# Making the negated DFT tables on GpSimd from the finished tables, behind the loads of batch 0

## The chip, the cores and the metric

The kernel runs on one core of a Trainium2 chip. Times are device microseconds of one execution of the whole program, as median of several executions. Before the change it was 611.16 us (610.72 to 611.26, 3 runs). Engines: PE is TensorE, PEld its weight loads, DVE is VectorE, ACT is ScalarE, POOL is GpSimd, SP issues DMAs.

## The reference

```python
# q, k, v: 8 batches, 12 heads, 448 positions, 64 per head
scores = scale * np.matmul(q, k.transpose(0, 1, 3, 2))
attn   = np.matmul(np.maximum(scores, 0.0) ** 2 / S, v)      # relu squared, no softmax
x      = attn.transpose(0, 2, 1, 3).reshape(B, 448, 768)
X      = np.fft.fft(np.fft.fft(x, axis=1), axis=2)
u      = x + np.real(X)
un     = (u - mean) / np.sqrt(var + 1e-06)                   # over the 768 channels
out    = u + np.maximum(un @ w_ch1, 0.0) @ w_ch2             # w_ch1: 768 x 3072
```

## The kernel before

Both Fourier transforms are matmuls with tables of cosines and sines, which the kernel makes itself in its first 30 us: a sequence table `seq` (128 x 2 x 2 x 240), its negated sine `nseq`, three channel tables `chan[m]` (128 x 2 x 386) and their negated sine halves `chan_neg`. DVE reduces the angles, ACT takes the sines. I call "stage 0" the stretch in which this goes on beside the attention of batch 0 and its first transform.

The kernel is not written in the order in which it runs. Each piece is a generator that asks for time on an engine, `need(engine, duration, dependencies, buffers)`. A scheduler on the host with a model of the durations lets them go in the order of their modelled starts, and that order is what is emitted for every engine. A change of one `need` can therefore reorder all engines.

```python
def build_dft():
    ...
    def turns(f, g, cols, rows, n, i):                 # the "reductions", on DVE
        r = work.tile([128, 2 * KH], mybir.dt.int32, name="dftr", ...)
        nc.vector.tensor_scalar(r[:, :n], cols, rows, None, op0=ALU.mult)
        nc.vector.scalar_tensor_tensor(f, cols, rows, r[:, :n], op0=ALU.mult, op1=ALU.subtract)
        nc.vector.scalar_tensor_tensor(g, f, -1.0, f, op0=ALU.mult, op1=ALU.max)
    def sine(dst, y, n, e, sign=1, bias=zero_t):
        e = yield need("ACT", act(n), [e + LATENCY["DVE"]])
        nc.scalar.activation(dst, y, AF.Sin, bias=bias, scale=sign * 2.0 * math.pi)
        dft_ready.t = e + LATENCY["ACT"]
    ...
    yield from sine(seq[:, 1, :, :]..., f[:, :2 * SX], 2 * SX, e)
    yield from sine(nseq...,            f[:, :2 * SX], 2 * SX, e, -1)      # negated: a third sine
    for m in range(3):
        e = yield need("DVE", 1.5, [indices_ready])
        y = work.tile([128, 4 * KH], FP32, name="dfty", ...)
        turns(...)
        yield from sine(chan[m][:, 0, :], y[:, 0:2 * KH], 2 * KH, e, -1, halfpi)
        yield from sine(chan[m][:, 1, :], y[:, 2 * KH:], 2 * KH, e)
        e = yield need("DVE", 0.3, [dft_ready])                           # negated: on DVE
        nc.vector.tensor_scalar(chan_neg[:, m], chan[m][:, :, KH:], -1.0, None, op0=ALU.mult)
        dft_ready.t = e + LATENCY["DVE"]
```

DVE's other work in stage 0 is the attention itself: it copies transposed q and k out of PSUM (`qkT`), squares ACT's relu of the scores in place, and makes two "folds" of every block of the result. The last two kinds read two operands from SBUF (a square reads its operand twice); the two `scalar_tensor_tensor` of the reductions above do so as well. Squares and folds are:

```python
nc.vector.tensor_tensor(r, r, r, op=ALU.mult)                                    # square
nc.vector.tensor_tensor(f[:, 0, :], x[:, 0:NS], x[:, XH:XH + NS], op=ALU.add)    # folds
nc.vector.tensor_tensor(f[:, 1, :], x[:, 0:NS], x[:, XH:XH + NS], op=ALU.subtract)
```

TensorE gets filler matmuls with zeros (tile `warm`) where the model thinks that it would idle. In `first_channels` the folds are multiplied with the channel tables.

Of the kernel before, what the change touches and what calls it, by code (L numbers as in the profile page):

```python
# [12 lines left out]
ALU = mybir.AluOpType  # L13
# [46 lines left out]
LATENCY = {"PE": 0.28, "ACT": 0.18, "DVE": 0.16, "POOL": 0.2, "SP": 0.1}  # L60
# [53 lines left out]
def need(eng, dur, deps=(), bufs=(), ok=None):  # L114
    return eng, dur, list(deps), list(bufs), ok


def mm(n):
    return n / 2400 + 0.006


def act(n):
    return n / 1200 + 0.2
# [14 lines left out]
def kernel(  # L138
# [9 lines left out]
    nc = tc.nc  # L148
# [8 lines left out]
    KH = D // 4 + 1  # L157
# [5 lines left out]
    SX = 240  # L163
# [19 lines left out]
    sch = Streams()  # L183
# [51 lines left out]
    seq = const.tile([128, 2, 2, SX], BF16, name="seqm")  # L235
    nseq = work.tile([128, 2, SX], BF16, name="nseq", tag="qs", bufs=1)
    chan = [const.tile([128, 2, 2 * KH], BF16, name=f"chan{m}") for m in range(3)]

    chan_neg = work.tile([128, 3, 2, KH], BF16, name="channeg", tag="xn", bufs=1)
    dft_ready, indices_ready = Cell(), Cell()  # L240

    def build_dft():
        row, col, col2 = drow, dcol, dcol2

        def turns(f, g, cols, rows, n, i):

            r = work.tile([128, 2 * KH], mybir.dt.int32, name="dftr", tag=f"pc{TC[i][0]}", bufs=1)
# [9 lines that stand above are left out]
        e = yield need("DVE", 0.3, [indices_ready])  # L257
        nc.vector.tensor_scalar(row[:, 0:2], row[:, 0:2], 1.0 / S, None, op0=ALU.mult)
        nc.vector.tensor_scalar(row[:, 4:7], row[:, 4:7], 1.0 / D, None, op0=ALU.mult)

        e = yield need("DVE", 2.1, [indices_ready])
        f = work.tile([128, 4 * KH], FP32, name="dfty", tag="u", bufs=2)
        g = work.tile([128, 4 * KH], FP32, name="dfty", tag="u", bufs=2)
        for i in range(2):
            turns(f[:, i * SX:(i + 1) * SX], g[:, i * SX:(i + 1) * SX], col[:, 0:SX], row[:, i:i + 1], SX, i)
        yield from sine(seq[:, 0, :, :].rearrange("p a s -> p (a s)"), g[:, :2 * SX], 2 * SX, e, -1, halfpi)
        yield from sine(seq[:, 1, :, :].rearrange("p a s -> p (a s)"), f[:, :2 * SX], 2 * SX, e)
        yield from sine(nseq.rearrange("p a s -> p (a s)"), f[:, :2 * SX], 2 * SX, e, -1)

        for m in range(3):  # L270
            e = yield need("DVE", 1.5, [indices_ready])
            y = work.tile([128, 4 * KH], FP32, name="dfty", tag="u1" if m < 2 else "o", bufs=2)
            turns(y[:, 2 * KH:], y[:, 0:2 * KH], col2, row[:, 4 + m:5 + m], 2 * KH, m % 2)
            yield from sine(chan[m][:, 0, :], y[:, 0:2 * KH], 2 * KH, e, -1, halfpi)
            yield from sine(chan[m][:, 1, :], y[:, 2 * KH:], 2 * KH, e)
            e = yield need("DVE", 0.3, [dft_ready])
            nc.vector.tensor_scalar(chan_neg[:, m], chan[m][:, :, KH:], -1.0, None, op0=ALU.mult)
            dft_ready.t = e + LATENCY["DVE"]


    GRP = 4 * R * HG * Dh * 4
# [155 lines left out]
    first_folds, f_ready, first_scores, first_mixed = [], [Cell() for _ in range(MC)], Cell(), Cell()  # L437
# [507 lines left out]
    def first_channels(i, ms):  # L945

        n0, n1 = TC[i]
        for m in ms:
            e = yield need("PE", 4 * mm(KH), [f_ready[m], dft_ready] + ([first_scores] if i else []),
                           [BS] if i and m == 0 else [])  # L950
            if i and m == 0:
                first_pps[i] = BS.take()
            for t in range(2):
                parts = [(0, 2 * KH, chan[m][:, t, :])] if m < 3 else \
                    [(0, KH, chan[m - 3][:, t, 0:KH]), (KH, 2 * KH, chan_neg[:, m - 3, t, :])]
                for c0, c1, tab in parts:
                    nc.tensor.matmul(first_pps[i][:n1 - n0, t, c0:c1], lhsT=first_folds[m][:, t, n0:n1], rhs=tab,  # L957
                                     start=(i == 1 and m == 0), stop=(m == MC - 1 and c1 == 2 * KH))
        if m < MC - 1:
            sch.add(first_channels(i, [MC - 1]), (0, 0))  # L960
        else:
            first_chan[i].t = e
            if all(c.t for c in first_chan):
                BXN.free.append(e)
# [170 lines left out]
    with tc.manual_schedule():  # L1135
        small_constants()
        sch.engine.update(POOL=0.5, DVE=0.8)

        sch.add(loading(), (0, 4))
        sch.add(build_dft(), (0, 0.5))  # L1140
        sch.add(turning(), (2, 2))
        sch.add(ffns(), (4, 0))
        sch.add(mixes(), (1, 1))
        sch.add(attention(0), (0, 0))
        for i in range(2):
            sch.add(first_channels(i, range(MC - 1)), (5, 5))
        sch.add(attentions(), (3, 3))
        sch.add(warming(), (9, 9))
        sch.run()
# [30 lines left out]
```

## Time and profile before

| | before |
|---|---|
| median of 3 runs | 611.16 us |
| span of the profiled run | 610.0 us |
| TensorE busy | 98% |
| DVE busy between 16 and 32 us | 15.45 of 16 us |
| first square on ACT starts (used below as the start of stage 0) | 9.68 us |
| first transform is copied out (tile `pc`, used as its end) | 41.05 us |

The prediction shows and reads the lines of this profile. In a timeline line the columns are start, time in us, engine, source line, operation, tiles, shapes, count and, in brackets, the idle time before it and what ended it. Two marks from ACT's timeline matter later: the copy of the first transform, and the first relu of the feed-forward layer (`hT`).

```profile
41.05 1.02 ACT L994 CAST pc<-psS 128x772 bf16<-128x772 f32 x1 [1.00 <-PE psS L957]
...
57.73 0.49 ACT L1063 ACTIVATE hT<-psF 128x384 bf16<-128x384 f32 x1 [2.33 <-PE psF L1090]
```

### The profile page before, as it was taken

What the parts mean: (1) busy time and instruction counts of PE and PEld (TensorE: products, weight loads), DVE (VectorE), ACT (ScalarE), POOL (GpSimd) and SP (SyncE); (2) the same over time, 40 slices, a digit from 0 to 9 for tenths busy, and PEclk for the clock granted to TensorE, in tenths of its full rate; (3) what the DMA queues carried; (4) which work ended last, traced back from release to release, by engine and by line L of the source; (5) the groups of instructions that cost most, each with busy time, mean ns of one, the idle gap of its engine ahead of it and who ended that gap; (6) DMA issues with size and microseconds to landing.
All of it is one profiled execution on the core that took longest, in us unless ns stands there. A gap on an engine that the chain in (4) does not pass through costs nothing.

```text
span 610.0 us, 10248 instructions
## 1 busy us (share of the span) xinstructions
PE 597.8 (98%) x4044; PEld 330.6 (54%) x4063; DVE 331.7 (54%) x767; ACT 315.6 (52%) x470; POOL 126.8 (21%) x175
## 2 busy tenths in 40 slices
PE   8998999999999999999999999999999999999997
PEld 6566556544455565555445565555445565554464
DVE  5966776965576768555744368545742447110011
ACT  5965772488555668536763167635782247114300
POOL 8432031411142124211420115210410004000000
PEclk9998999999999999999999999999999999999999
DMA  9999998965938995976496775985461225320022
GB/s 125 207 209 228 207 179 126 203 118 101 148 120 166 197 166 168 172 137 120 158 140 115 134 126 173 167 156 96 146 134 61 86 51 177 102 94 23 0 78 78
DMA packets 125216, 82.22 MB, mean 135 GB/s; under 512 B 76272, under 2 KB 113168, under 8 KB 125168
## 3 DMA queue, kind: packets, MB, share of 16 engines
q0 software_dynamic: 40320, 34.07, 35.3%
q1 hardware_dynamic: 84848, 47.50, 32.1%
q8 instruction: 32, 0.52, 0.3%
q14 instruction: 16, 0.13, 0.1%
HBM read 62.91 MB, written 26.69 MB: 147 GB/s over the span
## 4 chain that ended last, share of the span: by engine, by line
PE 84%; DVE 6%; ACT 5%; SPq 2%; issue 1%; DMA 1%; DVEq 0%; ACTq 0%
PE psF L1108 32%; PE psF L1090 31%; PE psF L524 7%; PE psS L538 6%; PE psS L982 2%; PE psS L1130 2%; ACT sq L558 2%; DVE stats L864 1%; PE psS L832 1%; ACT un L878 1%; SPq L923 1%; DMA o<-ubot 1%; PE psS L957 1%; PE psF L421 1%; ACT hT L1063 1%
## 5 line engine op out<-in xcount | busy, mean ns | idle before, releaser
L1090 PE MATMUL psF<-unT,w 128*128 128x384 bf16 (+1 forms) x1134 | 228.4, 353 | 2.2 <-ACT hT L1063 1.1
L558 ACT ACTIVATE sq<-psS 112x896 bf16<-112x896 f32 x192 | 165.3, 915 | 116.2 <-PE psS L538 116.2
L1108 PE MATMUL psF<-w,hT 128*128 128x384 bf16 (+2 forms) x1343 | 224.8, 326 | 0.1
L1108 PEld LDWEIGHTS <-hT 128*128 128x128 bf16 x1344 | 129.3, 98 | 92.4 <-issue 8.8
L1090 PEld LDWEIGHTS <-w 128*128 128x128 bf16 x1152 | 109.5, 98 | 111.6 <-issue 15.4
L1063 ACT ACTIVATE hT<-psF 128x512 bf16<-128x512 f32 (+1 forms) x180 | 98.2, 547 | 98.8 <-PE psF L1090 97.7
L564 DVE TENSOR_TENSOR sq<-sq 112x896 bf16<-112x896 bf16 x192 | 115.4, 619 | 48.5 <-ACT sq L558 46.9
L1071 DVE TENSOR_TENSOR o<-psF,o 128x384 f32<-128x384 f32 (+2 forms) x56 | 31.0, 554 | 109.8 <-PE psF L1108 108.5
L445 DVE TENSOR_SCALAR xT<-psF 128x224 bf16<-128x224 f32 x48 | 18.7, 390 | 74.7 <-PE psF L524 74.7
L538 PE MATMUL psS<-qkT 64*112 64x448 bf16 x384 | 52.6, 367 | 0.6 <-ACT qkT L426 0.4
L300 POOL DMA_DIRECT2D vn<-in_v_dram x24 | 17.3, 720 | 172.7 <-PE psF L524 154.1
L524 PE MATMUL psF<-sq,vn 112*64 112x448 bf16 x384 | 45.5, 358 | 1.4 <-DVE o L1071 0.5
L852 POOL TENSOR_TENSOR u<-tp,xn 128x385 f32<-128x385 f32 (+1 forms) x14 | 17.3, 1236 | 105.1 <-DVE tp L843 91.6
L538 PEld LDWEIGHTS <-qkT 64*112 64x112 bf16 x384 | 20.4, 125 | 27.9 <-issue 22.7
L878 ACT ACTIVATE un<-u,nmr,rstd 128x768 bf16<-128x768 f32 (+1 forms) x28 | 28.2, 1021 | 6.7 <-DVE nmr L873 6.7
L524 PEld LDWEIGHTS <-vn 112*64 112x64 bf16 x384 | 18.3, 109 | 23.1 <-issue 14.5
L864 DVE BATCH_NORM_STATS2 stats<-u 128x6 f32<-128x384 f32 (+1 forms) x56 | 28.1, 540 | 0.0
L900 POOL DMA_INDIRECT ubot<-u,back x16 | 16.8, 1048 | 43.3 <-DVE sq L564 27.5
L1130 PE MATMUL psS<-warm 128*128 128x126 bf16 (+1 forms) x210 | 18.9, 242 | 1.3 <-DVE warm L215 1.3
L300 POOL DMA_DIRECT2D qn<-in_q_dram x21 | 15.3, 728 | 23.1 <-DVE sq L564 9.2
L900 POOL DMA_INDIRECT nbot<-un,back x12 | 11.7, 972 | 35.6 <-ACT un L878 31.9
L452 DVE TENSOR_SCALAR xT<-psF 128x224 bf16<-128x224 f32 x47 | 18.0, 384 | 0.0
(119 smaller groups left out, 363.5 us busy)
## 6 DMA issues: line engine op xcount, KB each, us to landing
out_dram<-o SPq DMA_DIRECT2D x27, 384.0 KB, 2.6
vn<-in_v_dram POOLq DMA_DIRECT2D x24, 224.0 KB, 4.5
qn<-in_q_dram POOLq DMA_DIRECT2D x21, 224.0 KB, 6.3
kn<-in_k_dram POOLq DMA_DIRECT2D x21, 224.0 KB, 6.9
w<-in_moe_w_ch_dram POOLq DMA_DIRECT2D x12, 384.0 KB, 13.5
w<-in_moe_w_ch_dram POOLq DMA_DIRECT2D x4, 1152.0 KB, 23.4
utop<-u SPq DMA_DIRECT2D x8, 384.0 KB, 2.6
o<-utop SPq DMA_DIRECT2D x8, 384.0 KB, 3.5
```

The lines of the kernel that those rows point to most:

```text
L300: nc.gpsimd.dma_start(out=t, in_=src[b, hs].rearrange("h (p j) d -> p h (j d)", j=4))
L524: nc.tensor.matmul(av[h * Dh:(h + 1) * Dh, 0:S], lhsT=vn[:, c, h0 + h, :], rhs=sq[:, h, :], start=(c == 0), stop=(c == 3))
L538: nc.tensor.matmul(sc[:R, h, 0:S].rearrange("k (c q) -> k c q", c=4), lhsT=kT[ps, m % 2, c, :], rhs=qT[ps, m % 2], start=True, stop=True)
L558: nc.scalar.activation(r, sc[:R, :, 0:S], AF.Relu)
L564: nc.vector.tensor_tensor(r, r, r, op=ALU.mult)
L864: nc.vector.bn_stats(stats[:n, hf, :], u[:n, hf * (D // 2):(hf + 1) * (D // 2)])
L878: nc.scalar.activation(un[:n], u[:n], AF.Identity, bias=nmr[:n, i:i + 1], scale=rstd[:n, i:i + 1])
L1063: nc.scalar.activation(h[:, 0:N], ph[:, 0:N], AF.Relu)
L1071: nc.vector.tensor_tensor(o[:, hs], pc[:, 0:w], o[:, hs], op=ALU.add)
L1090: nc.tensor.matmul(ph[:, 0:N], lhsT=w1_sb[m][hf][:, jj * 128:(jj + 1) * 128], rhs=unT[:, m, 0:N], start=(m == 0), stop=(m == MC - 1))
L1108: nc.tensor.matmul(pc[:, 0:w], lhsT=hT[j][:, c * 128:(c + 1) * 128], rhs=w2_sb[j // 6][:, j % 6, hs], start=(j == 0), stop=(j == JC - 1))
L1130: nc.tensor.matmul(first_pps[0][:, t, c0:512], lhsT=warm[:, 0:128], rhs=warm[:, c0:512], start=not begun, stop=False)
```

## The change

The intent is to take a sine from ACT and three negations from DVE, both close to full in stage 0, and give them to POOL. POOL makes all four negated tables from the finished ones, not earlier than 18 us of the model, when the loads of batch 0 have been issued. Four cells keep the matmuls with the channel tables from being planned before.

```diff
+    negs_ready = [Cell() for _ in range(4)]
+    def negate(dst, src, t):
+        e = yield need("POOL", 0.55, [t, 18.0])
+        nc.gpsimd.tensor_scalar(dst, src, -1.0, None, op0=ALU.mult)
+        [c for c in negs_ready if c.t is None][0].t = e + LATENCY["POOL"]
 ...
-        yield from sine(nseq.rearrange("p a s -> p (a s)"), f[:, :2 * SX], 2 * SX, e, -1)
+        sch.add(negate(nseq, seq[:, 1], dft_ready.t), (1, 1))
 ...
-            e = yield need("DVE", 0.3, [dft_ready])
-            nc.vector.tensor_scalar(chan_neg[:, m], chan[m][:, :, KH:], -1.0, None, op0=ALU.mult)
-            dft_ready.t = e + LATENCY["DVE"]
+            sch.add(negate(chan_neg[:, m], chan[m][:, :, KH:], dft_ready.t), (1, 1))
 ...   # in first_channels
-            e = yield need("PE", 4 * mm(KH), [f_ready[m], dft_ready] + ([first_scores] if i else []),
+            e = yield need("PE", 4 * mm(KH), [f_ready[m], dft_ready] + negs_ready + ([first_scores] if i else []),
```

## The prediction

> **What bounds the kernel now.** I read the page first, then the windows of its first hundred microseconds (the change touches only tables made there), then the chain of waits and the timelines of those microseconds.
>
> ```profile
> PE 597.8 (98%) x4044; PEld 330.6 (54%) x4063; DVE 331.7 (54%) x767; ACT 315.6 (52%) x470; POOL 126.8 (21%) x175
> ...
> L1130 PE MATMUL psS<-warm 128*128 128x126 bf16 (+1 forms) x210 | 18.9, 242 | 1.3 <-DVE warm L215 1.3
> ```
>
> TensorE is busy 98% of 610 us, so only what shortens TensorE's queue, or a wait in front of it, counts. But 210 of its matmuls multiply zeros: fillers (tile warm) that the kernel's own list scheduler puts where its model thinks TensorE would idle. In the first 41 us a busy TensorE is therefore no proof that it is the bound; nor, once emitted, are fillers free: they keep their place in the queue.
>
> The windows of stage 0 (attention of batch 0 and its first transform); columns are stretch, length, then busy us and count of PE, PEld, DVE, ACT, POOL, then clock, DMA share, GB/s:
>
> ```profile
> 8.00:16.00 8.00, 7.41 (x126) 5.39 (x120) 6.51 (x13) 7.31 (x11) 6.73 (x24) 1.00 1.30 163
> 16.00:24.00 8.00, 7.60 (x83) 4.34 (x82) 7.66 (x20) 7.23 (x11) 4.58 (x10) 1.00 1.31 204
> 24.00:32.00 8.00, 7.99 (x87) 4.43 (x85) 7.79 (x21) 7.13 (x10) 2.11 (x4) 1.00 1.09 213
> 32.00:41.00 9.00, 8.91 (x112) 6.00 (x111) 6.20 (x15) 5.20 (x7) 3.67 (x5) 1.00 1.08 211
> ```
>
> From 16 to 32 us DVE is busy 15.45 of 16 us, ACT 14.36, TensorE 15.59 with fillers: three engines nearly balanced, so taking work from one gives only what the next lets through. The chain of waits in time order shows where ACT and DVE carry the end:
>
> ```profile
> 9.68 3.34 ACT sq L558 x4
> 13.01 1.02 ACT chan L254 x2
> 14.03 0.02 issue
> 14.05 0.27 DVE channeg L277
> 14.32 0.41 DVE dftr L248
> ...
> 15.97 0.55 DVE qkT L426
> ```
>
> From 9.68 to 16.52 the chain runs over ACT, one negation on DVE (the very work that moves), the next table's reductions, and a copy. From 16.56 on it is TensorE almost without a break until 34.89, one ACT wait of 0.93 us, and TensorE again to 41.02.
>
> **What the Trainium skill says.** "SBUF — State Buffer", section "Who interferes with whom": DVE and GpSimd share a port pair as an exclusive lock; a DVE instruction with two SBUF inputs contends with a GpSimd instruction that reads SBUF, and the loser waits. The trace agrees:
>
> ```profile
> 14.75 0.62 DVE L249 SCALAR_TENSOR_TENSOR dfty<-dcol,drow,dftr 128x386 f32<-128x386 f32 x1
> 14.86 0.62 POOL L231 TENSOR_SCALAR backv<-backv 128x1 f32<-128x1 f32 x1
> 15.41 0.56 DVE L250 SCALAR_TENSOR_TENSOR dfty<-dfty 128x386 f32<-128x386 f32 x1
> 15.56 0.46 POOL L232 TENSOR_TENSOR backv<-backv 128x1 f32<-128x1 f32 x1
> 16.09 0.18 POOL L233 CAST back<-backv 128x1 int32<-128x1 f32 x1
> ```
>
> One column on POOL takes 0.62 us, ending at 15.48, just after the DVE instruction that ends at 15.37; the next takes 0.46, ending at 16.02 after DVE's 15.97; alone one takes 0.18. Here POOL lost; it can as well be DVE that loses.
> "GPSIMD Engine Reference", section 4.1, calls one-input elementwise work on GpSimd "roughly line-rate". The trace agrees: a 128x768 scale-and-shift there takes 0.98 us.
> "TensorE: Matmul & The Clock Gate", section "What's actually happening": the clock halves after an idle window of about 3.4 us, windows free-running. In windows of 3.413 us the trace has, right after a window with TensorE busy 1.68 of 3.41 us (51.09 to 54.50), exactly one at half clock:
>
> ```profile
> 54.50:57.91 3.41, 3.21 (x24) 0.50 1.24 206
> ```
>
> **The change part by part.**
> Removed from ACT: the third sine of the sequence tables, 0.68 us by its row, about 0.6 by the spacing of starts. It lay just before ACT's first squares, but those started at 9.68 when the scores ended at 9.65, so its end (9.48) held nothing up: 0 us there.
> Removed from DVE: three negations of 0.254 to 0.265 us, some 0.2 us each by spacing, 0.6 us in all, in the stretch where DVE is 97% busy. The first is on the chain (0.27 us), and so is its wait for ACT's chan sines.
> Added to POOL: four negations. From 0.98 us for 768 columns and 0.18 for one, about 1.04 ns a column: 0.68 us (480 columns) and three of 0.58 (386), 2.4 us. In the built kernel POOL's queue is: three w loads, two negations, three loads, one, three loads, one, the rest. Before, POOL idled ahead of those loads 0.51, 0.64, 0.64, 0.63, 1.31, 1.31, 1.38, 1.31 us, waiting for slots of older DMAs. The first two negations (1.26 us, against 0.51 idle behind the fourth load) delay one load by 1.3 us, the next by 0.85 and the third by 0.2; the other two fit whole. Those weights are not used before 55.6 us and landed about 13.5 us after issue: 0 on the path.
> Consumers: the negated channel tables are first read at 32.27 us, nseq at 42.6. POOL has them by about 28: no wait.
> Moved: this is the larger part, since the scheduler orders everything anew. The instruction order of the built kernel differs from the old one only up to the first transform; from there TensorE, ACT, DVE and SP run the same order. In it:
> ACT takes the second qkT copy of group 0 before its first squares (at 13.90 before), then six squares before the first chan sines instead of four. TensorE's fillers between the first scores and the first transform are 150 instead of 146: 4 x 0.055 = +0.2 us. The first channel matmuls go later. DVE does the copy of group 1 before the reductions for the second channel table.
> I walked the new queues by hand with the durations and spacings above (squares 0.835 us apart on ACT, 0.53 on DVE; reductions 1.6 us; fold with its copies 1.17; two scores 0.33 on TensorE, 16 transposes 0.52, values 0.88; each score waits for the bank of the square two before; k of group 1 landed at 13.2, as POOL's wait shows). Early on it gains: sixth square done at 15.0 instead of 17.0. It then gives this back: the reductions for the second and third channel table now come just ahead of ACT's sines, which wait for them (17.3 and 22.8 us); square 15 starts at 27.25 against 26.78 before; squares 23 and 24 start at 34.9 and 35.7, as before; the last values end at 39.3 against 39.21, and the first transform at 41.1 against 41.02. Sum: **about +0.1 us**, with an error of my walk of half a microsecond or more either way. The lock adds to it: the first two POOL negations (about 18 to 19.4 us) meet folds and squares with two SBUF inputs; if DVE loses both it is 1.3 us late where it is full, of which my walk passes on up to 0.8. I add 0.1 to 0.2.
> After 41 us nothing changes in order and TensorE waits little, so the shift is carried to the end.
>
> **The rivals.**
> (a) The relief gets through: TensorE's waits of stage 0 go away. They were 0.16, 0.42 and 0.37 us between 9.7 and 17, and some 0.4 for a bank at 35.5, 1.35 in all; less 0.2 of fillers, the floor is −1.15 us: 610.0. For it: the first negation and its wait are on the chain. Against it: ACT's sines now wait for later reductions.
> (b) The bound becomes DVE with the lock: +1 us or so, 612. For it: DVE 97% busy and POOL's 0.62 us row. Against it: POOL may be the loser, and has slack.
> (c) The half-clock window moves. TensorE's busy share there is 49%; a stage 0 shorter by 1 us puts the same windows at 2.15 of 3.41 (63%), and at 77% none was throttled. If it escapes, up to 1.7 us more go (half of 3.41): 608.5. A later stage 0 keeps the share near 50%, so the window stays.
> (d) Late weights stall the first feed-forward stage. For it: loads move behind compute instructions on POOL. Against it: 25 us of slack and a queue of transfers always full (DMA share over 1 from 16 to 60 us).
>
> **Range and chances.** The reference is the median of 611.16 (610.72 to 611.26). The walk's +0.1 with 0.15 for the lock, less a little for rival (a), gives 611.3. Rival (a) alone sets the low end near 610, (a) with part of (c) 609.6; (b) the high end, 612.5. All of stage 0 that could move is a microsecond or two, 0.3% of the time; 2% would be 12 us. Hence within 2%: 0.98.
>
> **What would show it.** Right: negations of about 0.6 us on POOL between 18 and 28 us, w loads late by up to 1.3 us and no wait for them on TensorE; no nseq on ACT; ACT idle before the sines of the second and third channel table (17.3, 22.8); the last values matmul ending at 39 to 40 us and the pc copies starting at 40.5 to 42; one half-clock window near 54.5. Wrong: a first transform ending before 40 (relief passed through), DVE folds or squares stretched well beyond 0.3 and 0.62 us beside the negations (the lock is dearer), no half-clock window or a second one, or any difference after 60 us that is not a plain shift.

## The result, and the profile after

| | before | changed |
|---|---|---|
| median (range, runs), same rounds | 611.21 us (610.72 to 611.57, 4) | 612.91 us (611.58 to 613.67, 4) |
| span of the profiled run | 610.0 | 611.8 |
| first square on ACT, to the first transform's copy | 9.68 to 41.05: 31.37 | 9.60 to 43.40: 33.80 |
| first relu of the feed-forward layer | 57.73 | 58.75 |

The ratio changed to before is 1.0026, with a 95% interval of 1.0007 to 1.0045. Ratios here are the mean time of one kernel's fast runs over that of the other's fast runs of the same rounds, so not quite the ratio of the medians quoted. The change is slower by some 1.6 us: within 2%, and 0.4 us above the range that was predicted.

The page of the changed kernel says as little as before: TensorE 98% busy. POOL has 5.7 us more, four instructions for 5.4 of them, where 2.4 was predicted for them.

```profile
PE 597.4 (98%) x4048; PEld 330.1 (54%) x4067; DVE 333.2 (54%) x764; ACT 315.0 (51%) x469; POOL 132.5 (22%) x179
```

The windows of stage 0, columns as in the prediction, show where it went:

```profile
8.00:16.00 8.00, 7.74 (x111) 4.79 (x109) 6.83 (x13) 7.66 (x11) 6.88 (x25) 1.00 1.27 159
16.00:24.00 8.00, 6.49 (x73) 4.37 (x74) 7.79 (x14) 5.24 (x7) 7.97 (x11) 0.84 1.33 204
24.00:32.00 8.00, 8.00 (x88) 4.57 (x87) 7.35 (x18) 6.83 (x10) 4.31 (x7) 0.95 1.08 212
```

From 16 to 24 us DVE is a little fuller than before (7.79 us against 7.66) but completes 14 instructions where it completed 20. TensorE has 1.5 us of idle time, and its clock, 1.00 before, is 0.84 and 0.95. There are two effects to separate, and the timelines show both. First DVE and POOL of the changed kernel:

```profile
17.62 0.67 DVE L466 TENSOR_TENSOR fold<-xT 128x225 bf16<-128x225 bf16 x1
18.21 0.65 DVE L467 TENSOR_TENSOR fold<-xT 128x225 bf16<-128x225 bf16 x1
18.78 1.75 DVE L570 TENSOR_TENSOR sq<-sq 112x896 bf16<-112x896 bf16 x2
20.46 0.61 DVE L432 COPY qkT<-psF 128x896 bf16<-128x896 bf16 x1
20.99 1.45 DVE L570 TENSOR_TENSOR sq<-sq 112x896 bf16<-112x896 bf16 x2
22.36 0.49 DVE L256 TENSOR_SCALAR dftr<-dcol,drow 128x386 int32<-128x386 f32 x1
```

```profile
18.07 1.50 POOL L247 TENSOR_SCALAR nseq<-seqm 128x480 bf16<-128x480 bf16 x1
19.55 1.19 POOL L247 TENSOR_SCALAR channeg<-chan 128x386 bf16<-128x386 bf16 x1
...
22.36 1.53 POOL L247 TENSOR_SCALAR channeg<-chan 128x386 bf16<-128x386 bf16 x1
...
25.79 1.20 POOL L247 TENSOR_SCALAR channeg<-chan 128x386 bf16<-128x386 bf16 x1
```

In the kernel before, the same DVE work looked like this:

```profile
18.34 0.28 DVE L460 TENSOR_TENSOR fold<-xT 128x225 bf16<-128x225 bf16 x1
18.53 0.27 DVE L461 TENSOR_TENSOR fold<-xT 128x225 bf16<-128x225 bf16 x1
18.72 1.69 DVE L564 TENSOR_TENSOR sq<-sq 112x896 bf16<-112x896 bf16 x3
```

A fold takes 0.67 us where it took 0.28, a pair of squares 1.75. One thing doesn't fit exactly: unstretched, the first fold would have ended at 17.90, before the first negation starts at 18.07 in the profile. Spans on POOL are rough; I count this fold to the negations because it takes 0.28 us when memsets stand in their place (below). The copy `qkT`, whose source is PSUM, takes its usual 0.61. The negations take 1.2 to 1.5 us for a predicted 0.58 and 0.68. No run has one of them alone, but over all traces those of 386 columns never take less than 1.18, and they take 1.23 us with DVE's two-operand instructions beside them for 0.51 us (at 15.23 us, second trace of the old order below) as for all of it (at 30.61 us, first trace). So most of this is probably their own time, and only the longer ones, up to 1.9 us, are held up. TensorE then waits for DVE's copy, and runs at half clock just after:

```profile
21.12 1.50 PE L530 MATMUL psF<-sq,vn 112*64 112x448 bf16 x8 [1.13 <-DVE qkT L432]
22.55 0.62 PE L544 MATMUL psS<-qkT 64*112 64x448 bf16 x2
23.11 1.84 PE L1136 MATMUL psS<-warm 128*128 128x126 bf16 x16
```

In windows of 3.41 us, the second row is the one with the idle time, the third the one at half clock (0.50):

```profile
14.55:17.96 3.41, 3.41 (x42) 2.17 (x39) 3.20 (x8) 3.06 (x6) 3.26 (x6) 1.00 1.46 194
17.96:21.37 3.41, 1.90 (x32) 1.43 (x32) 3.41 (x6) 2.53 (x4) 3.40 (x5) 1.00 1.43 203
21.37:24.78 3.41, 3.41 (x26) 2.11 (x22) 3.34 (x7) 1.45 (x3) 3.39 (x5) 0.50 1.09 211
```

ACT's marks, against those of before:

```profile
43.40 1.02 ACT L1000 CAST pc<-psS 128x772 bf16<-128x772 f32 x1 [1.00 <-PE psS L963]
...
58.75 0.49 ACT L1069 ACTIVATE hT<-psF 128x384 bf16<-128x384 f32 x1 [1.00 <-PE psF L1096]
```

The first transform is 2.35 us later, the first relu only 1.02 later. The wait before that relu is 1.00 us where it was 2.33: the half-clock window that before had from 54.50 to 57.91 us is not there in this run, which gives 1.33 us back. At about 205 us another 0.72 us is lost, at a wait of TensorE on `o` (1.1 us against 0.5). Together 2.35 − 1.33 + 0.72 = 1.74, and the spans differ by 1.8.

### The profile page after: what moved, and what is told of

Read it like the earlier page. It is cut to its first block, busy times and chain, and to the rows that moved or that the text cites. A ratio compares the mean times of both kernels' runs of the same rounds, so it can differ in the third digit from the quotient of the medians.

```text
span 611.8 us, 10252 instructions
## 1 busy us (share of the span) xinstructions
PE 597.4 (98%) x4048; PEld 330.1 (54%) x4067; DVE 333.2 (54%) x764; ACT 315.0 (51%) x469; POOL 132.5 (22%) x179
## 4 chain that ended last, share of the span: by engine, by line
PE 83%; DVE 7%; ACT 4%; DMA 3%; issue 1%; SPq 1%; POOL 0%; DVEq 0%; ACTq 0%; POOLq 0%
PE psF L1114 33%; PE psF L1096 32%; PE psF L530 7%; PE psS L544 6%; PE psS L988 2%; ACT sq L564 2%; DMA qkT<-qkr 1%; PE psS L838 1%; DVE stats L870 1%; PE psS L1136 1%; ACT un L884 1%; DMA vn<-in_v_dram 1%; PE psS L963 1%; DMA o<-ubot 1%; DVE sq L570 1%
## 5 line engine op out<-in xcount | busy, mean ns | idle before, releaser
L570 DVE TENSOR_TENSOR sq<-sq 112x896 bf16<-112x896 bf16 x192 | 116.8, 624 | 47.5 <-ACT sq L564 45.9
L858 POOL TENSOR_TENSOR u<-tp,xn 128x385 f32<-128x385 f32 (+1 forms) x14 | 17.3, 1237 | 105.1 <-DVE tp L849 91.6
```

## The experiments

The candidates for the cost were, in this order: **the lock**, POOL's reads of SBUF beside DVE's instructions with two SBUF operands; **the new order** of the instructions; and **the half clock**, a window at half speed that follows the gaps. Effects of a microsecond are at the edge of what timed rounds resolve here, so I time each version and also read from each trace the length of stage 0, from ACT's first square to the first transform's copy. A line that starts "+" or "−" is the edit against the kernel named.

**Negations replaced by memsets, in the changed kernel** (the result is wrong, relative error 0.21). Same order on TensorE, ACT and DVE, but POOL only writes. A memset is also shorter than a negation, so POOL's later loads come earlier as well.

```diff
-        nc.gpsimd.tensor_scalar(dst, src, -1.0, None, op0=ALU.mult)
+        nc.gpsimd.memset(dst, 0.0)
```

> Wrong result on purpose: the changed kernel with every instruction of TensorE, ACT and DVE in its order, but the four negations on POOL are memsets of the same tiles, which read nothing. Theory L (the lock: DVE's folds and squares lose the shared port to the negations, which read SBUF): the folds of 17.6 us go back from 0.67 to 0.28 us, TensorE's wait of 1.1 us before the values matmuls at 21 us goes, the first transform's copies start near 41.5 instead of 43.4, and the time is 610.5 to 611.5, some 1.5 us under the changed kernel's 612.9. Theory O (the new order of the streams costs it): nothing changes, 612.5 to 613.2.

> The memset kernel (wrong on purpose) once more: 31.59 us from first square to first copy with full clock from 7.1 us. Theory L: at any position of the windows at most 32.1, and no half-clock window before 50 us. Rival (the early full clock alone lengthens the stage in this order): 32.5 or more when full clock comes at 4.3 to 5.5 us.

Stage 0 took 31.59 and 31.48 us, the ratio to before is 0.9999 (0.9973 to 1.0025). DVE and POOL of the second trace:

```profile
17.50 0.28 DVE L466 TENSOR_TENSOR fold<-xT 128x225 bf16<-128x225 bf16 x1
17.70 0.27 DVE L467 TENSOR_TENSOR fold<-xT 128x225 bf16<-128x225 bf16 x1
17.88 1.16 DVE L570 TENSOR_TENSOR sq<-sq 112x896 bf16<-112x896 bf16 x2
18.95 0.62 DVE L432 COPY qkT<-psF 128x896 bf16<-128x896 bf16 x1
19.49 1.15 DVE L570 TENSOR_TENSOR sq<-sq 112x896 bf16<-112x896 bf16 x2
20.55 0.42 DVE L256 TENSOR_SCALAR dftr<-dcol,drow 128x386 int32<-128x386 f32 x1
```

```profile
17.92 0.53 POOL L247 MEMSET nseq<- 128x480 bf16 x1
18.35 0.46 POOL L247 MEMSET channeg<- 128x386 bf16 x1
```

From the first fold to the next reductions DVE needs 20.55 − 17.50 = 3.05 us; with negations on POOL it was 22.36 − 17.62 = 4.74. So two negations cost DVE 1.69 us, and the new order by itself costs nothing like it: without POOL's reads the whole loss is gone. POOL's loads, which moved too, are no rival: in stage 0 of the changed kernel TensorE waits only for the copy `qkT` (1.1 us) and for squares of ACT (0.6), never for a load, and the stretched instructions read SBUF alone. That is the lock (more exactly, reads by POOL; writes alone do no harm).

**The changed kernel again**, three more traces, to see what repeats.

> The changed kernel once more, for another position of the half-clock window (in the four traces so far the windows lie on a grid of 3.413 us whose phase differs from run to run) and for its time on the chip of the other runs. If the lock alone costs: even with the half-clock window elsewhere, folds at 17.6 us take about 0.67 us, TensorE waits about 1.1 us for a DVE copy near 21 us, and the copies of the first transform start at 41.7 to 42.5. If the window is what costs: without it in the first 40 us they start at 41.5 as with memsets. Time 612 to 613.

> One more look at the changed kernel. Both traces of it so far have a half-clock window inside the first stage (21.4 and 25.8 us), with 33.8 and 34.4 us from first square to first copy. Without one in the first stage the lock and the order alone should leave 32.3 to 33.1 us; with one 33.5 to 34.5.

> As after_3: without a half-clock window in the first stage 32.3 to 33.1 us from first square to first copy, with one 33.5 to 34.5.

The timed rounds of the first gave 614.16 us (613.08 to 615.16, 6 runs) against 611.93 (610.00 to 613.45, 11 runs), ratio 1.0040 (1.0019 to 1.0060): the change is slower, in a second session too. Stage 0 was 34.41, 32.95 and 35.78 us. These differ in half-clock windows: one, none and two. The first and the last are longer than was expected. The windows of the last, where the gaps leave TensorE busy for 1.81 us in the first row (why the clock stays at half for the third row, after a row that is busy throughout, isn't shown):

```profile
23.39:26.80 3.41, 1.81 (x26) 1.10 (x23) 3.31 (x9) 3.06 (x5) 3.39 (x6) 1.00 1.08 211
26.80:30.21 3.41, 3.41 (x19) 1.36 (x19) 2.71 (x8) 1.42 (x3) 1.24 (x3) 0.50 1.07 210
30.21:33.62 3.41, 3.41 (x20) 1.64 (x18) 1.71 (x3) 2.43 (x3) 0.27 (x1) 0.50 1.09 214
```

The trace without such a window shows the loss to the lock alone. It has the same gaps, but split over two windows (TensorE busy 2.76 and 2.26 of 3.41 us):

```profile
20.60 0.95 PE L530 MATMUL psF<-sq,vn 112*64 112x448 bf16 x8 [0.65 <-DVE qkT L432]
...
24.42 0.59 PE L427 MATMUL psF<-ident,qk 112*64 112x112 bf16 x16 [0.39 <-DVE xT L458]
25.78 0.40 PE L544 MATMUL psS<-qkT 64*112 64x448 bf16 x2 [0.77 <-ACT sq L564]
```

So 32.95 − 31.53 (mean of the two with memsets) = 1.4 us for the lock, and 0.3 to 2.9 us more when windows fall badly (table below). Whether they do differs from run to run.

The record has the granted clock of every timed run, which separates the two further. In the traces, a mean clock of 0.999 or 1.000 goes with no half-clock window before the last microseconds, 0.997 with one, 0.994 with two. Of the ten timed runs of the changed kernel four had none: 611.58 to 613.32 us, mean 612.68. Of the 47 timed runs of before in these sessions 17 had none: mean 610.69. So some 2 us are lost without any half clock. Counted this way the changed kernel had 0.9 windows per run and before 0.7, so the windows spread the times of both and can carry little of the difference in the mean (0.2 windows of at most 1.7 us each, half of 3.41).

**The order of before, with the negations on POOL.** The scheduler is left to plan the old sine and the old negations, so that TensorE, ACT and DVE keep their old order; only what is emitted changes.

```diff
-        yield from sine(nseq..., f[:, :2 * SX], 2 * SX, e, -1)
+        e = yield need("ACT", act(2 * SX), [e + LATENCY["DVE"]])      # planned, not emitted
+        dft_ready.t = e + LATENCY["ACT"]
+        sch.add(negate(nseq, seq[:, 1], 18.0), (1, 1))
-            nc.vector.tensor_scalar(chan_neg[:, m], chan[m][:, :, KH:], -1.0, None, op0=ALU.mult)
+            sch.add(negate(chan_neg[:, m], chan[m][:, :, KH:], e), (1, 1))
```

> The kernel before with TensorE, ACT and DVE in its own order, but the three negations leave DVE, the third sine leaves ACT, and POOL makes all four where they fell in its queue. Theory L: DVE instructions with two SBUF inputs beside the POOL negations stretch by 0.4 us and more, and the time is 611.5 to 613, at or above the 611.2 of before. Theory O: without the new order only the relief remains, 610 to 611.

> The fastest correct kernel so far once more (order of before, POOL negates). If its lead of 0.18 per cent is real: ratio 0.9975 to 0.9990 again. If it came from the lucky position of the half-clock window in its trace (full clock from 4.5 us instead of 6.7): ratio within 0.001 of 1.

Stage 0 took 31.25 and 31.22 us; ratios 0.9982 (0.9957 to 1.0008) and 0.9991 (0.9959 to 1.0022). The 611.5 to 613 that the lock theory expected was a miss, and the first run's lead in time shrank in the second. No loss, although POOL needed 1.2 to 1.9 us for each negation here as well. And with memsets in that same order (again wrong):

> Wrong result on purpose: as e2_before_order_pool, but memsets in place of POOL's negations, so that no lock on reads is possible. Relief alone: copies of the first transform at 39.5 to 40.1. If it equals e2's 40.06 within 0.2, the lock costs nothing in the order of before.

31.23 us, ratio 0.9976 (0.9957 to 0.9995). So in the old order the lock costs nothing that can be seen, and the relief of ACT and DVE by itself is worth 0.1 to 0.3 us of stage 0 (31.37 and 31.55 in the two traces of before, less 31.23). Why it costs nothing is in DVE's timeline. With memsets, DVE waits for ACT among its squares:

```profile
18.48 1.81 DVE L570 TENSOR_TENSOR sq<-sq 112x896 bf16<-112x896 bf16 x3
20.47 0.63 DVE L570 TENSOR_TENSOR sq<-sq 112x896 bf16<-112x896 bf16 x1 [0.18 <-ACT sq L564]
```

With the negations on POOL it doesn't:

```profile
17.61 2.62 DVE L570 TENSOR_TENSOR sq<-sq 112x896 bf16<-112x896 bf16 x4
```

From the first fold to the next reductions both take 2.91 to 2.92 us, and the third table's reductions end 13.03 and 13.00 us after the first square. The stretching fills time in which DVE would have waited. There is also less of it: four squares take 2.62 us here where the next four, at 22.90 us of the same trace, take 2.23, and the folds before them are not stretched. In the new order DVE lost 0.96 to 1.69 us in this stretch (four traces of the changed kernel), and had no wait to absorb it.

**Negations on DVE, in the new order.**

```diff
-        nc.gpsimd.tensor_scalar(dst, src, -1.0, None, op0=ALU.mult)
+        nc.vector.tensor_scalar(dst, src, -1.0, None, op0=ALU.mult)
```

> The changed kernel's order of all other instructions, but the four negations are put on DVE at the places in the program where POOL had them. Theory L: DVE pays four times about 0.2 us in its queue but loses no port; copies of the first transform start near 42, time 610.8 to 611.8. Theory O: 612.5 to 613.5.

Stage 0: 32.12 us; nothing stretched. The four negations take 0.25 to 0.32 us each. Against the memsets (31.53 on average) these four cost stage 0 0.6 us on DVE, and 1.4 us on POOL. The timed ratio, 1.0005 (0.9974 to 1.0036), doesn't resolve this; the profiled run lost 2.4 us at about 200 us, which hits other kernels to other amounts.

**Negations late on POOL**, planned for after 27 us, when fewer folds and squares are near, in the new order and in the old one.

```diff
-    def negate(dst, src, t):
+    def negate(dst, src, t, at):       # negs_ready is set first, then:
+        yield need("SP", 0.0, [at])    # at = 28.5 for nseq, (27.0, 28.0, 28.2)[m]
```

> The changed kernel, everything else in its order, but POOL's negations come after nearly all weight loads (about 28 to 34 us), where DVE has gaps. Theory L: no stretched DVE instruction between 17 and 24 us, first transform's copies at 40.5 to 42, time 610 to 611.3, possibly the best of all. Theory O: 612.5 to 613.2.

> TensorE, ACT and DVE in the order of the kernel before, relieved of the negations, which POOL makes late (one before the last weight load, three after). If the order is what costs and the relief is worth 1 us: copies of the first transform at 39.8 to 40.5 (40.06 with the negations where they fell), time 610.3 to 611.2, no worse than that run. If the lock mattered in that order too: a further 0.3 to 0.6 us.

New order: 32.13 us, ratio 0.9999 (0.9975 to 1.0023). Nothing is stretched between 17 and 24 us, but the negations now meet the folds that TensorE waits for. One takes 0.89 us, and TensorE waits 0.4 us:

```profile
31.56 0.28 DVE L467 TENSOR_TENSOR fold<-xT 128x225 bf16<-128x225 bf16 x1
31.75 0.89 DVE L468 TENSOR_TENSOR fold<-xT 128x225 bf16<-128x225 bf16 x1
```

Old order: 31.64 us (0.9990, 0.9972 to 1.0008), 0.4 worse than the early negations in that order. Later is better in the one order, worse in the other. Both expectations were missed: 612.2 us for the expected 610 to 611.3, and 0.4 us worse for "no worse". It depends on what the negations meet.

**Every negation twice, in the changed kernel**, as a test whether the loss grows with the count.

> Dose: the changed kernel with each of POOL's four negations made twice in a row. Theory L: about twice the DVE delay; copies of the first transform 0.8 us or more later than the changed kernel's for the same number of half-clock windows (45 and later with one in the stage, 43.3 and later with none), time 613 to 616. If DVE's loss of the port does not matter: within 0.3 us of the changed kernel.

A miss: 32.75 us, no more than with four (32.95). Ratio 1.0007 (0.9955 to 1.0060). The eight took 1.2 to 1.8 us each. DVE lost 3.81 − 3.05 = 0.76 us from first fold to third reductions, less than in any trace with four (4.01 to 4.74 there, less the same 3.05): one fold took 1.02 us, but both pairs of squares their usual 1.15. Later squares were stretched too (2.53 us for four at 29.35 us), which is the 0.2 us by which this version stands out in the table below. So the loss is not a price per negation; it is decided by which DVE instructions they meet, and when.

**Only the later channel matmuls gated.** The change planned all channel matmuls after the negations; only those of the blocks from 3 on need them.

```diff
-   [f_ready[m], dft_ready] + negs_ready + ...
+   [f_ready[m], dft_ready] + (negs_ready if m >= 3 else []) + ...
```

> The changed kernel, but only the channel matmuls that read the negated tables are held back for them in the scheduler's model, so the first channel matmuls go out earlier. If the gate on all channel matmuls is what spoiled the order: copies of the first transform at 41 or earlier without a half-clock window before them. If the new order of ACT and DVE and the lock are what costs, no better than the changed kernel: copies at 41.7 to 42.5, more with a half-clock window, time 612 to 613.5.

32.30 us, ratio 1.0008 (0.9977 to 1.0040). Here the negation of `nseq` meets the second table's reductions, one of which takes 1.30 us where it usually takes 0.56. TensorE's waits move to the folds instead of going away:

```profile
PE psS L963 <- DVE fold L466: 1.3, 2, 0.8
```

**Fillers in the gaps, in the changed kernel**: 16 filler matmuls ahead of the values matmuls that waited for `qkT`, and in the second version 14 more ahead of the later score that waited for ACT.

```diff
+  for _ in range(16 if b == 0 and ma == 1 else 0):     # second version: also 14 if b == 0 and i == 13
+      nc.tensor.matmul(first_pps[0][:, 0, 2 * KH:512], lhsT=warm[:, 0:128], rhs=warm[:, 2 * KH:512],
+                       start=False, stop=False)
```

> The changed kernel with 16 more zero matmuls (0.88 us) just before the second values matmuls, where TensorE waited 1.1 us for DVE. Theory C (the gap drops TensorE's activity in one clock window and so halves the clock for the next): no half-clock window before 50 us in the trace, copies of the first transform at 41.7 to 42.3, time 611.5 to 612.3. Rival: the fillers only lengthen TensorE's queue, 613 or more.

> As e8_fill, with 14 further zero matmuls (0.77 us) before the thirteenth score, where the trace of that run showed the second gap of 0.77 us; work that fills gaps only. Theory C: with both gaps filled no half-clock window falls before 50 us in any run, and copies of the first transform come near 42.5, as in e8_fill; mean time 0.3 to 1 us under the changed kernel's. Rival: the fillers lengthen the queue, and copies come at 43 or later.

No half-clock window in stage 0 in either; lengths 32.88 and 33.82 us, ratios 1.0029 (1.0006 to 1.0051) and 1.0030 (0.9987 to 1.0073). The second seems to say that the fillers lengthen TensorE's queue, but that would be a wrong reading: 0.81 us of its excess is a wait for a load of k at 13.4 us, ahead of all fillers, which the trace of the first doesn't have. The fillers themselves stand where TensorE would wait. As a test of the half clock both are weak, since one trace of the unfilled kernel has no window either, and the times didn't improve.

**The kernel before against itself**, as a control.

> The kernel before, submitted as if it were a change: the ratio to itself must hold 1, and its interval tells what this machine can resolve (about 0.2 to 0.3 per cent). Its trace shows the first stage at another position of the half-clock windows: 31.2 to 31.5 us from the first square to the first copy if the start of TensorE's full clock does not matter to that length.

Ratio 1.0001 (0.9966 to 1.0037); stage 0 31.55 us. So timed ratios within about 0.35% of 1 cannot be told from none in such rounds, and single runs of before range from 609.7 to 617.5 us over the sessions. The change's first 1.0026 would be weak evidence alone; its second session (1.0040) and its traces carry it.

**The third table's sines moved behind three more squares, in the changed kernel.** In the traces of the new order the loss looked as if ACT passed it on: its sines wait for DVE's reductions (up to 1.41 us) and hold back the squares behind them.

```diff
-  yield from sine(chan[m][:, 0, :], y[:, 0:2 * KH], 2 * KH, e, -1, halfpi)
+  yield from sine(chan[m][:, 0, :], y[:, 0:2 * KH], 2 * KH, e if m < 2 else max(e, 24.5), -1, halfpi)
```

> The changed kernel, but the two sines of the third channel table are placed three squares later on ACT (after eight squares more, not five), so that they no longer stand in front of a square that TensorE's scores wait for. In the traces of the changed order the length of stage 0 is the time at which DVE ends the reductions of the third channel table plus 18.85 us wherever no half-clock window lies in it. Theory 'through ACT': the lateness reaches TensorE because ACT, in order, waits for these reductions before its sines and keeps the next squares back. Then stage 0, at about 14.05 us for the end of the reductions after the first square, comes down from 32.9 to about 31.5 us, as with the memsets, and the wait of 0.8 us for ACT's square near 25.7 us is gone. Rival 'directly': TensorE's transposes wait for a PSUM bank that DVE frees only after the same reductions (0.4 to 0.8 us of wait for xT at about 24.3 us). Then only the 0.77 us of wait for the square goes: 32.2 us. If neither binds, 32.9. A half-clock window in stage 0 adds 0.3 to 1.5 us, two of them 2.9, and is subtracted in reading. Of the median: about 611 to 612.

> A second trace of the same kernel, to see whether the length of stage 0 repeats within 0.2 us and whether a half-clock window occurs in it. Theory of the half clock: with a gap of 0.8 us less near 25 us, no window before it falls below 1.9 of 3.41 us busy, so none occurs; if one occurs in both traces, the gaps before 22 us suffice by themselves.

Stage 0 took 34.00 us in the first trace, which lost 1.1 us to a load of k at its start, and 32.82 in the second: no gain. Ratio 1.0008 (0.9933 to 1.0083). ACT's wait for the reductions is gone, and TensorE now waits longer, for DVE itself, shown here from the second trace:

```profile
23.61 0.40 PE L544 MATMUL psS<-qkT 64*112 64x448 bf16 x2 [0.28 <-ACT sq L564]
...
26.46 0.95 PE L530 MATMUL psF<-sq,vn 112*64 112x448 bf16 x8 [1.26 <-DVE qkT L432]
```

So it isn't ACT, and my size for the direct path, 32.2, was too low as well: DVE's own queue sets the end. The table lists for the traces in the new order when DVE ends the third reductions, counted from the first square on ACT.

| version in the new order | third reductions end after | stage 0 | difference | half-clock windows in stage 0 |
|---|---|---|---|---|
| memset, two traces | 12.63, 12.74 | 31.48, 31.59 | 18.85, 18.85 | 0 |
| on DVE | 13.27 | 32.12 | 18.85 | 0 |
| later channel matmuls gated (TensorE's order differs) | 13.55 | 32.30 | 18.75 | 0 |
| doubled | 13.67 | 32.75 | 19.08 | 0 |
| fillers | 14.02 | 32.88 | 18.86 | 0 |
| changed, third trace | 14.09 | 32.95 | 18.86 | 0 |
| sines later, two traces | 14.04, 15.20 | 32.82, 34.00 | 18.78, 18.80 | 0 |
| more fillers | 14.93 | 33.82 | 18.89 | 0 |
| changed, first trace | 14.62 | 33.80 | 19.18 | 1 |
| changed, second trace | 14.02 | 34.41 | 20.39 | 1 |
| changed, fourth trace | 14.03 | 35.78 | 21.75 | 2 |
| late on POOL | 12.71 | 32.13 | 19.42 | 0, but a fold stretched at 31.75 |

Wherever there is no half clock and no later stretching, stage 0 is the end of those reductions plus 18.75 to 19.1 us, over a range of 2.6 us. Every tenth that DVE loses before is lost by stage 0. The half clock comes on top, 0.3, 1.5 and 2.9 us. It occurs in 3 of 4 traces of the changed kernel and in none of the 16 traces of the other versions, before included, so it goes with the gaps; by the granted clock 7 of the changed kernel's 12 runs had a half-clock window at any place.

No correct version beat both kernels beyond doubt. The best candidate is the old order with the negations on POOL, whose two intervals both include 1.

## Why the prediction was right or wrong

**What was right.** The verdict, within 2%; that the order changes up to the first transform only; that nobody waits for the negated tables or for the weights behind them on POOL (a load came late by up to 2.6 us for a predicted 1.3, and TensorE had no wait for one); and that ACT waits for the reductions ahead of its third pair of sines near 22.8 us (the profile: 23.7 in the second trace of the changed kernel, 22.3 with memsets; the second pair, foreseen at 17.3, shows no wait). Rival (a), relief that gets through, is small at most: 0.1 to 0.3 us in the old order. Rival (d), late weights, didn't occur. The walk through the new queues said +0.1 us for order and relief. The two memset traces of the new order give 31.53 against 31.37, +0.16. That closeness is partly luck: the walk claimed no better than half a microsecond, and the two traces of before differ by 0.18.

**What was wrong: the term for the lock.** This is the step that failed. It was "if DVE loses both it is 1.3 us late where it is full, of which my walk passes on up to 0.8. I add 0.1 to 0.2." Both halves of the doubt were resolved the wrong way: that DVE might not be the loser, and that only part would be passed on. The mechanism and, for DVE, the size were right (1.3 us foreseen, 1.4 in the trace without half clock), the size partly by luck, since the negations are longer than was assumed and DVE waits for part of their length only. DVE lost 1.69 us in the profiled run between the first fold and the third reductions, and it passed on all of it, as the table above shows: third reductions at 14.62 instead of 12.68 us are 1.94 us of stage 0. The negations also took twice the time that a row of one column and one of 768 gave them; the row "alone" of 0.18 us was a cast, not the same operation. (In the queue of POOL, 1.26 − 0.51 is 0.75 and not 0.85, and in rival (c) 610.0 − 1.7 is 608.3; neither matters.) The last values matmul ended at 41.57 us and the copy of the first transform started at 43.40, outside the 39 to 40 and 40.5 to 42 that were to show the step right, while folds and squares "stretched well beyond 0.3 and 0.62 us" are the sign that was named for it being wrong. Rival (b), "DVE with the lock: +1 us or so, 612", is what happened. The reason that was given against it, POOL may be the loser and has slack, carried no weight: DVE loses as well, and POOL's slack doesn't help DVE.

**What was wrong: the half clock.** "A later stage 0 keeps the share near 50%, so the window stays" failed twice. In the profiled run the window near 54.5 us wasn't there, which gave back 1.33 us. It is absent from the second trace of before as well (full clock from 4.20 us there, from 6.74 in the first); what decides isn't shown. And a new one appeared in stage 0, because gaps of 0.38 and 1.13 us fell into one window (3.41 − 1.51 = 1.90 us busy). "No half-clock window or a second one" had been named as a sign of a wrong prediction, but without any weight in the sum.

**What was wrong: nothing changes after 41 us but a shift.** The order doesn't, but the clock near 55 us (−1.33) and a wait at about 205 us (+0.72) did, and both vary between runs of one kernel.

The sum for the profiled pair, in the prediction's steps: start of the first square −0.08, order and relief +0.16 (predicted +0.1), lock +1.94 (predicted 0.1 to 0.2), half clock in stage 0 +0.33 (predicted 0; it is what the others leave of the 2.35), the lost window near 54.5 us −1.33 (0), the wait near 205 us +0.72 (0). Together +1.74 of the 1.8 by which the spans differ. That the loss repeats is shown by the second session's +0.40% and by the runs without any half clock, some 2 us apart.

## What to carry to other kernels

Moving elementwise work from DVE to POOL need not be relief when DVE has instructions with two SBUF operands at that time: here stage 0 lost 1.4 us to it, more than twice the 0.6 us that the work cost on DVE. Before a move, look at what will lie beside it and whether the engine that may be stretched has waits to absorb it; the same four negations were free in one order and cost 1.4 us in the other. And when a term of a sum is uncertain and sits on a full engine, give it its full size in the range.

## What the Trainium skill lacked or had wrong

- "SBUF — State Buffer", section "Who interferes with whom", is right that DVE instructions with two SBUF inputs contend with GpSimd instructions that read, and not with those that only write: memsets on POOL left a fold at 0.28 us, negations stretched it to 0.67. The page's section "Summary: rules for kernel authors" says that the second of the two to issue fully blocks until the first finishes. That isn't what these traces show: DVE lost 1.69 us beside two negations of 2.69 us together, and in the doubled kernel two squares took their usual 1.15 us (from 18.81 us) beside negations that ran from 18.13 to 21.23 us. The loss didn't grow with POOL's work: eight negations cost stage 0 no more than four (32.75 and 32.95 us).
- "GPSIMD Engine Reference", section 4.1, calls one-input work "roughly line-rate". Beside DVE's work of stage 0 that didn't hold: 386 bf16 columns took 1.2 to 1.8 us, where 768 columns from fp32 to bf16 took 0.98 us near 50 us. No run has such a negation alone, but 1.23 us with DVE's two-operand instructions beside it for only 0.51 us says that contention is not the whole reason.
- "TensorE: Matmul & The Clock Gate", section "What's actually happening", says that the half clock comes after at least one idle window. Windows with TensorE busy 1.81 and 1.90 of 3.41 us were enough here, while one of 1.72 us, from 53.07 to 56.48 us in the second trace of the changed kernel, was not. The page gives no busy share, and these runs don't give a clean one either. Its free-running window fits: the end of the cold start differs between 4.2 and 7.2 us from run to run.
